# A recurrence of weighted keys and two feed-forward layers: the bonus term moved onto the diagonal of A, and the state product cut into strips of 32

## The chip, the core and the metric

The kernel runs on one core of a Trainium2 chip. The metric is the device time of one execution in microseconds (us); smaller is better. The core has a matrix engine (TensorE, PE in the rows), a vector engine (VectorE, DVE), a scalar engine (ScalarE, ACT), a general one (GpSimd, POOL) and a queue that issues transfers (SyncE, SP). Matrix products land in PSUM, everything else lives in SBUF.

## The reference

Four batches, eight heads, 768 steps, head size 48. For each head a state of 48 x 48 decays, takes up the outer product of the step's key and value, and is read by the step's r. The key and value of the step itself count with a bonus factor u:

```python
for t in range(S):
    cur = np.einsum('bhd,bhe->bhde', u[None] * kt, vt)
    y[:, :, t] = np.einsum('bhd,bhde->bhe', rt, state + cur)
    state = wt[:, :, :, None] * state + np.einsum('bhd,bhe->bhde', kt, vt)
```

The 3072 x 384 result goes through a feed-forward layer, `(h * clip(h + 3, 0, 6) / 6) @ w_out` with `h = x @ w_in` (2048 wide), and then through a second one, `((x @ w1) * (x @ w2)) @ w3 @ w_out` (1024 wide). All is float32.

## The kernel before

**The recurrence by units.** The 768 steps are cut into six chunks of 128. A unit is one chunk of one batch: unit `uu` is chunk `uu // 4` of batch `uu % 4`, 24 units in all. Inside a unit the recurrence is written as products. VectorE scans the decays (`P`, `F`) and scales K and R by them (`K`, `R`). TensorE makes the scores `s` (line 304), K^T R for each of the eight heads, 128 x 128 each, in two PSUM tiles. ScalarE copies them to an SBUF tile A (`a`, `b`, line 311) and GpSimd sets all that isn't strictly above the diagonal to zero (`c`, `d`, line 315). TensorE then adds the outputs of the unit in one PSUM tile (`o`, line 369) from three parts: the state's share R x St, the bonus share, and the share A x V.

**The bonus share.** For the step itself the output gets v times the sum over d of r u k. GpSimd multiplies r by u (`u`, line 402) and by k (`v`, line 404), VectorE sums over d (`l`, line 336: one factor `al` per step and head), GpSimd multiplies V by that (`w`, line 339), and TensorE adds this to the output by a product with the identity (line 377: 12 strips of 32 columns).

**The state.** K is transposed on TensorE (`n`, line 292) and copied (`m`). The state's change is K^T V for each pair of heads (`t`, line 348): one product 112 x 96, of which only the two diagonal blocks of 48 x 48 are used. VectorE adds them to the state (`y`, line 359), which GpSimd decays (`T`).

**Strips.** A product of `o` writes 32 partitions of PSUM, and four in a row write the four quarters. A float32 product stands as two instructions in the trace.

**The first feed-forward layer** runs with the units of the recurrence: block `G` is 9 products of 512 columns (lines 182 to 184) for one of 16 slices of one chunk, `E`, `M`, `H`, `L` are its relu on ScalarE, its product on VectorE, the copy of its high part on ScalarE and the rest on GpSimd (line 451), and `B` is 9 products with w_out. For the first 16 slices the weights are also converted on the way (`a`, `d`, `i`, `p`; lines 166, 170, 796, 802).

**Order.** Nothing is scheduled: the table `ORDER` is a list of such letters, and each engine's queue holds its part of it in that order. PSUM tiles named `wk` rotate through three buffers, so the fourth `wk` tile waits until the first was read. After the table the rest of layer one, a product of w3 and w_out, and layer two follow (phases that the change doesn't touch).

Of the kernel before, what the change touches and what calls it, by code (L numbers as in the profile page):

```python
# [8 lines left out]
F32 = mybir.dt.float32  # L9
# [3 lines left out]
BF16 = mybir.dt.bfloat16  # L13
FP16 = mybir.dt.float16
U16 = mybir.dt.uint16
ALU = mybir.AluOpType
ACTF = mybir.ActivationFunctionType
PSUM = bass.MemoryType.PSUM
# [4 lines left out]
def kernel(  # L23
# [15 lines left out]
    nc = tc.nc  # L39
# [7 lines left out]
    H, D = u.shape  # L47
    DM, NT = out.shape
    G, UPB, BP, C = rT.shape
    S = UPB * C  # L50
    B = NT // S
    NP = H // 2
# [13 lines left out]
    NB2 = NT // N2  # L66
    LAG = 2
    ORDER = (
# [30 lines left out]
    )  # L99
    NST = 3  # L100
    KA = 13
    LO1 = 2
    NZ = 2
    ZC = 2 * DM
    X1F = 13
    LO = 'w0 k0 r0 w1 k2 r1 w3 k1 n0 n3 r2 w2 k3 n1 r3 n2 s0'
    XE = 'ppv'
    XP = (14, 15, 15)
    XL = 13
# [5 lines left out]
    const = ctx.enter_context(tc.tile_pool(name="const", bufs=1))  # L115
# [2 lines left out]
    c_all = const.tile([128, NU, NP], F32, name="c_all")  # L118
    ones = const.tile([128, 1], F32, name="ones")
    flag = const.tile([1, 1], I32, name="flag")  # L120

    main = ExitStack()
    st_p = ctx.enter_context(tc.tile_pool(name="stage", bufs=NST))
# [6 lines left out]
    def pst(tag):  # L130
        return ps.tile([128, 512], F32, tag=tag, name=tag, bufs={"h": 2, "acc": 3, "wk": 3}[tag])
# [8 lines left out]
    wt = wkv.enter_context(tc.tile_pool(name="wk_t", bufs=1, side="right"))  # L140
# [58 lines left out]
    nat3 = ep.tile([128, 2 * DM + VW], F32, name="nat3")  # L199
    qT = [ep.tile([128, FL], F32, name=f"q{q}") for q in range(2)]  # L200
    ubk = ep.tile([128, H], F32, name="ubk")
    St = [wp.tile([128, NP, 2 * D], F32, name=f"St{b}") for b in range(B)]
    xT = {}
    U = [{} for _ in range(NU)]
# [46 lines left out]
    def unit(uu):  # L251
# [3 lines left out]

        d = U[uu]
        c, b = divmod(uu, B)
        first, last = c == 0, c == UPB - 1
        W, kt, rt = (t[own(uu)] for t in (Wb, Kb, Rb))
        kh, rh = (t.rearrange("p (a c) -> p a c", a=NP) for t in (kt, rt))  # L260
        rows = lambda t: t.rearrange("p (m c) -> p m c", c=C)
# [51 lines left out]
        def a_mask(h2):  # L313
            A = d["A"][:, :, h2]
            nc.gpsimd.affine_select(out=A, in_=A, compare_op=ALU.is_ge, fill=0.0, base=-1, pattern=[[0, NP], [1, C]],  # L315
                                    channel_multiplier=-1)

        def q_t():
            nc.gpsimd.tensor_tensor(qT[uu % 2][0:G], kt[0:G], rt[0:G], op=ALU.mult)

# [21 lines left out]
            nc.gpsimd.tensor_tensor(St[b][0:G], St[b][0:G], cs.unsqueeze(2).to_broadcast([G, NP, 2 * D]), op=ALU.mult)  # L342

        def state():
            d["pu"] = pst("acc" if first else "wk")
            for pr in range(NP):
                ds = slice(pr * 2 * D, (pr + 1) * 2 * D)
                nc.tensor.matmul(d["pu"][0:G, ds].rearrange("p (j e) -> p j e", j=2), d["kn"][:, pr, :], d["nv"][:, :, pr, :],  # L348
                                 start=(pr == 0), stop=(pr == NP - 1), skip_group_check=True)
            release("n", uu)  # L350

        def state_add():
            pv = d.pop("pu")[:, 0:DM].rearrange("p (a e) -> p a e", e=2 * D)
            for h2 in range(2):
                rs, es = slice(64 * h2, 64 * h2 + D), slice(h2 * D, (h2 + 1) * D)
                if first:
                    nc.scalar.activation(out=St[b][rs, :, es], in_=pv[rs, :, es], func=ACTF.Copy)
                else:
                    nc.vector.tensor_tensor(St[b][rs, :, es], St[b][rs, :, es], pv[rs, :, es], op=ALU.add)

        def outputs():


            px = d["px"] = pst("wk")
            seen = set()

            def strip(q, lhs, rhs):
                m, j = divmod(q, 4)
                nc.tensor.matmul(px[32 * j:32 * j + 32, m * C:(m + 1) * C], lhs, rhs, start=j not in seen, stop=False, skip_group_check=True)  # L369
                seen.add(j)  # L370

            if not first:
                for q in range(3 * NP):
                    pr, i = divmod(q, 3)
                    strip(q, St[b][0:G, pr, 32 * i:32 * i + 32], rh[0:G, pr, :])
            for q in range(3 * NP):
                strip(q, flat(d["nr"])[:, 32 * q:32 * q + 32], ident)
            for q in range(3 * NP):
                pr, i = divmod(q, 3)
                strip(q, d["v64"][:, i // 2, pr, (0, 32, 32)[i]:(32, 64, 64)[i]],  # L380
                      d["A"][:, pr, i // 2])
            for pr in range(NP):
                strip(3 * pr + 1, d["v64"][:, 1, pr, 0:32], d["A"][:, pr, 1])
            load_r(after(uu))
            release("n", uu)

        def x_split(part):
# [7 lines left out]
                nc.vector.tensor_tensor(xl, pxv, xh.bitcast(F32), op=ALU.subtract)  # L395

        G_, V_ = nc.gpsimd, nc.vector
        return {
            "P": scan_p, "K": lambda: mul_k(V_), "k": lambda: mul_k(G_), "F": scan_f, "R": lambda: mul_r(V_),
            "r": lambda: mul_r(G_), "n": k_t, "m": k_n, "s": scores, "a": lambda: a_copy(0), "b": lambda: a_copy(1),  # L400
            "c": lambda: a_mask(0), "d": lambda: a_mask(1),
# [3 lines left out]
            "V": lambda: V_.tensor_tensor(d["nr"], d["nr"], d["nk"], op=ALU.mult),  # L405
            "q": q_t, "e": q_alpha, "l": alpha, "w": q_bonus if first else bonus, "T": decay, "t": state, "y": state_add, "o": outputs,
            "g": lambda: x_split(0), "h": lambda: x_split(1)}


    wio_t = [[wio_p.tile([128, KA, 2 * DM], F32R, name="wio" + q) for q in "hl"]]  # L410
# [397 lines left out]
    if True:  # L808
# [7 lines left out]
        nc.scalar.activation(out=ones, in_=ones, func=ACTF.Copy)  # L816
        nc.gpsimd.memset(Dp, 0.0)
        nc.gpsimd.memset(Df, 0.0)
        for t in Wb:
            nc.gpsimd.memset(t[0:G, PAD - 1:PAD], 0.0)  # L820
        for t in St:
# [30 lines left out]
        last = NB - 1  # L852
# [135 lines left out]
```

## Time and profile before

| | |
|---|---|
| median of 3 runs | 887.28 us (886.37 to 887.92) |
| profiled execution | 888.7 us, of which the span from first to last instruction is 887.0 us |
| TensorE busy | 865.2 us, 98% of the span |
| GpSimd, VectorE, ScalarE busy | 375.8, 357.5, 330.5 us |
| granted TensorE clock | 0.994 of full speed over the span |
| the units and the table `ORDER` | from the start to about 500 us |

Busy times are shares of one execution. Products overlap on TensorE, so the distance between the starts of two products tells what one costs, not its duration.

### The profile page before, as it was taken

The page shows a single profiled execution, that of the slowest core. Times are in us where ns is not written, and L with a number is a line of the kernel's source. Part 1 is how long each engine was busy: PE and PEld are TensorE (multiplying, and loading weights), DVE is VectorE, ACT ScalarE, POOL GpSimd, SP SyncE. Part 2 cuts the span into 40 slices and gives each one's busy share as a digit, 9 for nine tenths or more (in the row PEclk, how much of TensorE's full clock was granted, in tenths as well). Part 3 has the DMA queues.
Part 4 walks back from the last instruction along what each step waited for, and adds up shares of the span by engine and source line. Part 5 has one row for each costly group of instructions (what it writes and reads, how often), then busy time and mean ns, then how long its engine had stood idle before and what let it go on. Part 6 is the DMA issues. An engine that isn't in the chain of part 4 may idle for free.

```text
span 887.0 us, 13899 instructions
## 1 busy us (share of the span) xinstructions
PE 865.2 (98%) x5752; PEld 707.5 (80%) x5752; DVE 357.5 (40%) x537; ACT 330.5 (37%) x556; POOL 375.8 (42%) x337
## 2 busy tenths in 40 slices
PE   7999999999999999999999999899999999999997
PEld 6777677888888888888888888688888888888785
DVE  7799884444444444444213444155111111212110
ACT  1666633333333333343335555365222222222211
POOL 6677877464555555455232211224232222323221
PEclk9999999999999999999999999999999999999999
DMA  9756541212322122221203452560110404030001
GB/s 257 240 193 229 179 123 46 62 62 62 97 62 75 59 86 66 83 81 53 65 1 108 136 176 85 178 212 2 48 45 1 154 1 155 1 133 1 36 1 39
DMA packets 29239, 81.92 MB, mean 92 GB/s; under 512 B 3312, under 2 KB 3440, under 8 KB 29168
## 3 DMA queue, kind: packets, MB, share of 16 engines
q1 hardware_dynamic: 29168, 80.95, 27.9%
q8 instruction: 47, 0.77, 0.3%
q14 instruction: 24, 0.20, 0.1%
HBM read 71.50 MB, written 9.44 MB: 91 GB/s over the span
## 4 chain that ended last, share of the span: by engine, by line
PE 78%; issue 12%; POOL 5%; DVE 3%; ACT 1%; DMA 0%; SPq 0%; POOLq 0%; ACTq 0%; DVEq 0%
PE h L182 9%; PE acc L183 9%; PE acc L182 9%; PE acc L184 9%; PE h L184 9%; PE h L183 9%; PE wk L369 5%; PE wk L183 4%; PE wk L184 4%; PE wk L182 4%; POOL gl L451 4%; PE wk L304 3%; PE wk L348 1%; PE wk L292 1%; POOL A L315 1%
## 5 line engine op out<-in xcount | busy, mean ns | idle before, releaser
L451 POOL TENSOR_TENSOR gl<-t,gh 128x512 fp32r<-128x512 f32 x144 | 192.0, 1334 | 390.6 <-ACT gh L447 390.5
L447 ACT ACTIVATE gh<-t 128x512 fp32r<-128x512 f32 x144 | 91.0, 632 | 193.1 <-DVE t L606 105.9
L440 DVE SCALAR_TENSOR_TENSOR t<-t,h 128x512 f32<-128x512 f32 x96 | 65.3, 681 | 136.2 <-ACT t L435 135.8
L606 DVE TENSOR_TENSOR t<-t,wk 128x512 f32<-128x512 f32 x48 | 33.0, 687 | 202.9 <-PE wk L184 202.9
L435 ACT ACTIVATE t<-h 128x512 f32<-128x512 f32 x96 | 57.3, 597 | 136.8 <-PE h L184 125.1
L182 PE MATMUL h<-xh,wioh 128*128 128x512 f32 x234 | 94.9, 406 | 0.3 <-DVE t L440 0.3
L182 PE MATMUL acc<-gh,wioh 128*128 128x512 f32 x234 | 93.1, 398 | 0.0
L183 PE MATMUL acc<-gl,wioh 128*128 128x512 f32 x234 | 91.6, 392 | 1.0 <-POOL gl L451 1.0
L184 PE MATMUL h<-xh,wiol 128*128 128x512 f32 x234 | 92.2, 394 | 0.3 <-DVE wiol L802 0.3
L183 PE MATMUL h<-xl,wioh 128*128 128x512 f32 x234 | 91.7, 392 | 0.0
L184 PE MATMUL acc<-gh,wiol 128*128 128x512 f32 x234 | 91.4, 391 | 0.0
L605 ACT ACTIVATE t<-h 128x512 f32<-128x512 f32 x48 | 28.6, 596 | 99.6 <-PE h L184 99.6
L183 PE MATMUL acc<-gl,w34h 128*128 128x512 f32 x144 | 56.3, 391 | 0.0
L184 PE MATMUL acc<-gh,w34l 128*128 128x512 f32 x144 | 56.3, 391 | 0.0
L182 PE MATMUL acc<-gh,w34h 128*128 128x512 f32 x144 | 56.2, 390 | 0.0
L182 PEld LDWEIGHTS h<-xh,wioh 128*128 128x128 f32 x234 | 44.0, 188 | 11.7 <-issue 1.3
L184 PEld LDWEIGHTS h<-xh,wiol 128*128 128x128 f32 x234 | 43.9, 188 | 11.1 <-DVE wiol L802 1.3
L183 PEld LDWEIGHTS acc<-gl,wioh 128*128 128x128 f32 x234 | 44.0, 188 | 10.5 <-POOL gl L451 1.6
L184 PEld LDWEIGHTS acc<-gh,wiol 128*128 128x128 f32 x234 | 43.9, 188 | 9.5
L182 PEld LDWEIGHTS acc<-gh,wioh 128*128 128x128 f32 x234 | 44.0, 188 | 9.4 <-issue 0.2
L166 ACT ACTIVATE z<-st 128x768 f16<-128x768 bf16 (+2 forms) x46 | 41.2, 902 | 27.0 <-DVE st L170 8.5
L183 PEld LDWEIGHTS h<-xl,wioh 128*128 128x128 f32 x234 | 44.0, 188 | 8.5
(141 smaller groups left out, 1727.0 us busy)
## 6 DMA issues: line engine op xcount, KB each, us to landing
nat<-in_rkv_dram SPq DMA_DIRECT2D x20, 640.0 KB, 3.9
st<-in_wio_dram SPq DMA_DIRECT2D x16, 768.0 KB, 4.7
st<-in_w3T_dram SPq DMA_DIRECT2D x16, 512.0 KB, 4.4
W<-in_wT_dram SPq DMA_DIRECT2D x24, 224.0 KB, 2.7
K<-in_kT_dram SPq DMA_DIRECT2D x24, 224.0 KB, 2.6
R<-in_rT_dram SPq DMA_DIRECT2D x24, 224.0 KB, 3.0
st<-in_wT_dram SPq DMA_DIRECT2D x12, 448.0 KB, 6.0
x1d<-ev SPq DMA_DIRECT2D x18, 256.0 KB, 2.9
```

The lines of the kernel that those rows point to most:

```text
L166: nc.scalar.activation(out=z.bitcast(FP16).rearrange("p (n two) -> p n two", two=2)[:, :, 1], in_=half, func=ACTF.Copy)
L182: nc.tensor.matmul(ps_ap, lh, rh, start=first, stop=False)
L183: nc.tensor.matmul(ps_ap, lh, rl, start=False, stop=False)
L184: nc.tensor.matmul(ps_ap, ll, rh, start=False, stop=last)
L304: nc.tensor.matmul(d["sc"][h2][:, pr * C:(pr + 1) * C], kh[sl, pr, :], rh[sl, pr, :], start=(pr == 0), stop=(pr == NP - 1), skip_group_che ...
L369: nc.tensor.matmul(px[32 * j:32 * j + 32, m * C:(m + 1) * C], lhs, rhs, start=j not in seen, stop=False, skip_group_check=True)
L435: nc.scalar.activation(out=t, in_=hp[:, 0:N1], func=ACTF.Relu, bias=3.0)
L440: nc.vector.scalar_tensor_tensor(t, t, 6.0, hp[:, 0:N1], op0=ALU.min, op1=ALU.mult)
L447: nc.scalar.activation(out=gh, in_=t, func=ACTF.Copy)
L451: nc.gpsimd.tensor_tensor(gl, t, gh.bitcast(F32), op=ALU.subtract)
L605: nc.scalar.activation(out=a, in_=pp[0][:, 0:N2], func=ACTF.Copy)
L606: nc.vector.tensor_tensor(a, a, pp[1][:, 0:N2], op=ALU.mult)
```

## The change

The change has three parts.

First, for units 7 to 23 (`DG = 7`) the bonus factors go onto the diagonal of A. GpSimd fills the whole tile A with one select, which puts `al` on the diagonal and zero elsewhere (`c`, `a_diag`). VectorE then copies the scores over it where a constant mask `tri` is one, that is strictly above the diagonal, straight from PSUM (`a` and `b`, `a_over`). In these units the copies `a`, `b` on ScalarE, the two masks on GpSimd, the product `w` on GpSimd and the 12 identity strips of `o` are gone. Units 0 to 6 keep the old way.

Second, in all units the state's change `t` is computed by strips: for each pair of heads four products of 32, 16, 32 and 16 rows by 48 columns in place of one of 112 x 96.

Third, `ORDER` is new. From unit 6 on `t` of one unit, `o` of the next and `s` of the one after stand next to each other on TensorE, and `n` stands alone between two blocks. In the early part some of the work also changes its engine (`r0` moves to GpSimd, `r6` and `r7` move to VectorE), and the order of the first loads is another.

```diff
-        'K21 G R21 L P22 B E u22 M F22 H G v22 L l22 B E M T22 H w22 G L B E M H G L B E M H s20 V L V G V a20',
+        'L o17 y16 s18 g17 h17 G a18 b18 B E u19 M v19 H n17 G L m17 l19 c19 B E M H G K19 L R19 P20 B E M T20',
...
+    DG = 7
...
-    LO = 'w0 k0 r0 w1 k2 r1 w3 k1 n0 n3 r2 w2 k3 n1 r3 n2 s0'
+    LO = 'w0 k0 r0 r1 k1 w1 r2 w2 n0 k2 w3 n1 n2 r3 k3 n3 s0'
...
+        def a_diag():
+
+            d["A"] = wt.tile([128, NP, 2, C], F32, tag="A", name="A", bufs=2)
+            A = d["A"].rearrange("p a j c -> p (a j) c")
+            nc.gpsimd.affine_select(out=A, in_=d["al"].unsqueeze(2).to_broadcast([128, H, C]), compare_op=ALU.is_equal, fill=0.0, base=0,
+                                    pattern=[[0, H], [1, C]], channel_multiplier=-1)
+
+        def a_over(h2):
+
+            nc.vector.copy_predicated(d["A"][:, :, h2], tri.unsqueeze(1).to_broadcast([128, NP, C]),
+                                      d["sc"][h2].rearrange("p (a c) -> p a c", c=C))
...
             for pr in range(NP):
-                ds = slice(pr * 2 * D, (pr + 1) * 2 * D)
-                nc.tensor.matmul(d["pu"][0:G, ds].rearrange("p (j e) -> p j e", j=2), d["kn"][:, pr, :], d["nv"][:, :, pr, :],
-                                 start=(pr == 0), stop=(pr == NP - 1), skip_group_check=True)
+                for j in range(4):
+                    r0, r1 = 32 * j, (32, 48, 96, 112)[j]
+                    nc.tensor.matmul(d["pu"][r0:r1, pr * D:(pr + 1) * D], d["kn"][:, pr, r0:r1], d["nv"][:, j // 2, pr, :],
+                                     start=(pr == 0), stop=(pr == NP - 1), skip_group_check=True)
...
-            for q in range(3 * NP):
+            for q in range(0 if diag else 3 * NP):
                 strip(q, flat(d["nr"])[:, 32 * q:32 * q + 32], ident)
...
+        if diag:
+            ops.update(a=lambda: a_over(0), b=lambda: a_over(1), c=a_diag)
```

What moves is seen in the queues. On TensorE, before, around unit 17: the scores `s` (L304), the outputs `o` (L369) with `n` (L292) behind them, and the state's change `t` (L348) stand in three places, with blocks `G` (h<-) and `B` (acc<-) between them.

```order
L184 MATMUL acc<-gh,wiol 128x512
L304 MATMUL wk<-R_106,K_104 128x128 x8
L182 MATMUL h<-xh,wioh 128x512
...
L184 MATMUL acc<-gh,wiol 128x512
L369 MATMUL wk<-R_106,St_121 32x128 x12
L369 MATMUL wk<-ident,nat 32x128 x12
L369 MATMUL wk<-A,nat 32x128 x16
L292 MATMUL wk<-ident,K_104 128x112 x4
L182 MATMUL h<-xh,wioh 128x512
...
L348 MATMUL wk<-nat,kn 112x96 x4
L182 MATMUL acc<-gh,wioh 128x512
```

After the change (lines are those of the changed program: L364 is `t`, L385 `o`, L306 `s`) the same place of unit 17 reads so; the two rows of L364 stand eight times in turn.

```order
L185 MATMUL acc<-gh,wiol 128x512
L364 MATMUL wk<-nat,kn 32x48
L364 MATMUL wk<-nat,kn 16x48
...
L385 MATMUL wk<-R_107,St_123 32x128 x12
L385 MATMUL wk<-A,nat 32x128 x16
L306 MATMUL wk<-R_106,K_104 128x128 x8
L183 MATMUL h<-xh,wioh 128x512
```

The strips of unit 16's `t`, unit 17's `o` without its identity strips, and unit 18's `s` now follow each other with nothing between.

On VectorE, before, around the same unit: the split `h` (L395) of unit 17's output, then its `y` (L359), a product `M` (L440), and K, R and the scan P of the next unit.

```order
L395 TENSOR_TENSOR xl<-wk,xh 128x3x128
L359 TENSOR_TENSOR St_121<-St_121,wk 48x4x48 x2
L440 SCALAR_TENSOR_TENSOR t<-t,h 128x512
L278 TENSOR_TENSOR K_104<-K_104,P 112x4x127
L284 TENSOR_TENSOR R_106<-R_106,W_102 112x512
```

After the change `y` of unit 16 (L375) stands ahead of `h` of unit 17 (L411), and two masked copies of unit 18's scores (L329) follow.

```order
L274 SCALAR_TENSOR_TENSOR P<-W_103,Dp 112x512
L271 TENSOR_REDUCE c_all<-P 112x4
L276 RECIPROCAL Df<-c_all 112x4
L459 SCALAR_TENSOR_TENSOR t<-t,h 128x512
L283 SCALAR_TENSOR_TENSOR W_103<-W_103,Df 112x512
L459 SCALAR_TENSOR_TENSOR t<-t,h 128x512
L375 TENSOR_TENSOR St_122<-St_122,wk 48x4x48 x2
L411 TENSOR_TENSOR xl<-wk,xh 128x3x128
L329 COPY_PREDICATED A<-tri,wk 128x4x128 x2
```

What moved there: the read of `t`'s PSUM tile now comes while TensorE is at `o`, and the second score tile of `s` takes over that very buffer.

## Rows read from the trace of the kernel before

**Rows 1.** The page: busy times, and the chain that ended last.

```profile
PE 865.2 (98%) x5752; PEld 707.5 (80%) x5752; DVE 357.5 (40%) x537; ACT 330.5 (37%) x556; POOL 375.8 (42%) x337
...
PE 78%; issue 12%; POOL 5%; DVE 3%; ACT 1%; DMA 0%; SPq 0%; POOLq 0%; ACTq 0%; DVEq 0%
```

**Rows 2.** Timeline of TensorE, unit 17: start, duration, line, operation, count.

```profile
329.34 0.39 PE L184 MATMUL acc<-gh,wiol 128*128 128x512 f32 x1
329.66 1.16 PE L304 MATMUL wk<-R,K 48*128 48x128 f32 x16
330.75 0.50 PE L182 MATMUL h<-xh,wioh 128*128 128x512 f32 x1
331.09 0.39 PE L183 MATMUL h<-xl,wioh 128*128 128x512 f32 x1
...
334.52 0.39 PE L183 MATMUL acc<-gl,wioh 128*128 128x512 f32 x1
334.74 0.39 PE L184 MATMUL acc<-gh,wiol 128*128 128x512 f32 x1
335.06 0.86 PE L369 MATMUL wk<-R,St 112*32 112x128 f32 x24
335.74 0.84 PE L369 MATMUL wk<-ident,nat 128*32 128x128 f32 x24
336.40 1.06 PE L369 MATMUL wk<-A,nat 128*32 128x128 f32 x32
337.38 0.60 PE L292 MATMUL wk<-ident,K 112*128 112x112 f32 x4
337.76 0.48 PE L182 MATMUL h<-xh,wioh 128*128 128x512 f32 x1
338.07 0.39 PE L183 MATMUL h<-xl,wioh 128*128 128x512 f32 x1
...
339.68 0.39 PE L184 MATMUL h<-xh,wiol 128*128 128x512 f32 x1
339.91 0.93 PE L348 MATMUL wk<-nat,kn 128*112 128x96 f32 x8
340.63 0.48 PE L182 MATMUL acc<-gh,wioh 128*128 128x512 f32 x1
340.95 0.39 PE L183 MATMUL acc<-gl,wioh 128*128 128x512 f32 x1
```

**Rows 3.** Timeline of TensorE, a transpose that stands alone between products.

```profile
49.40 0.39 PE L184 MATMUL acc<-gh,wiol 128*128 128x512 f32 x1
49.63 0.55 PE L292 MATMUL wk<-ident,K 112*128 112x112 f32 x4
...
50.26 0.39 PE L183 MATMUL acc<-gl,wioh 128*128 128x512 f32 x1
```

**Rows 4.** Busy time by stretch: us, PE, PEld, DVE, ACT, POOL, clock, DMA.

```profile
39.00:60.00 21.00, 20.95 (x183) 16.92 (x181) 18.64 (x23) 15.70 (x25) 14.94 (x12) 1.00 0.58 188
...
80.00:100.00 20.00, 18.37 (x164) 14.12 (x162) 18.97 (x22) 11.82 (x17) 14.51 (x13) 1.00 0.57 188
100.00:120.00 20.00, 18.68 (x160) 14.68 (x161) 16.56 (x21) 11.44 (x17) 15.08 (x12) 1.00 0.39 135
...
158.00:180.00 22.00, 22.00 (x195) 18.15 (x194) 9.57 (x16) 7.57 (x14) 11.93 (x12) 1.00 0.20 62
```

**Rows 5.** Groups by line: operation, count, busy us, mean ns, idle before.

```profile
L606 DVE TENSOR_TENSOR t<-t,wk 128x512 f32<-128x512 f32 x48 | 33.0, 687 | 202.9 <-PE wk L184 202.9
...
L284 DVE TENSOR_TENSOR R<-R,W 112x512 f32<-112x512 f32 x22 | 18.2, 829 | 0.0
...
L315 POOL TENSOR_SCALAR_AFFINE_SELECT A<-A 128x512 f32<-128x512 f32 x48 | 38.1, 816 | 10.0 <-ACT A L311 9.9
```

**Rows 6.** Timeline of VectorE after unit 17's state product.

```profile
340.88 0.72 DVE L359 TENSOR_TENSOR St<-St,wk 48x192 f32<-48x192 f32 x2 [2.27 <-PE wk L348]
```

**Rows 7.** Longest single wait of TensorE, 39 to 140 us: total, times, longest.

```profile
PE wk L369 <- POOL nat L339: 1.3, 1, 1.3
```

More of the change, by code (lines that the diff above doesn't have):

```diff
@@ L15 @@
 U16 = mybir.dt.uint16
+U8 = mybir.dt.uint8
 ALU = mybir.AluOpType
@@ L120 @@
     flag = const.tile([1, 1], I32, name="flag")
+    tri = const.tile([128, C], U8, name="tri")
     main = ExitStack()
@@ L201 @@
     ubk = ep.tile([128, H], F32, name="ubk")
+    pre = ep.tile([128, C], F32, name="pre")
     St = [wp.tile([128, NP, 2 * D], F32, name=f"St{b}") for b in range(B)]
@@ L257, in unit @@
         c, b = divmod(uu, B)
-        first, last = c == 0, c == UPB - 1
+        first, last, diag = c == 0, c == UPB - 1, uu >= DG
         W, kt, rt = (t[own(uu)] for t in (Wb, Kb, Rb))
@@ L346, in state @@
             for pr in range(NP):
-                ds = slice(pr * 2 * D, (pr + 1) * 2 * D)
-                nc.tensor.matmul(d["pu"][0:G, ds].rearrange("p (j e) -> p j e", j=2), d["kn"][:, pr, :], d["nv"][:, :, pr, :],
-                                 start=(pr == 0), stop=(pr == NP - 1), skip_group_check=True)
+                for j in range(4):
+                    r0, r1 = 32 * j, (32, 48, 96, 112)[j]
+                    nc.tensor.matmul(d["pu"][r0:r1, pr * D:(pr + 1) * D], d["kn"][:, pr, r0:r1], d["nv"][:, j // 2, pr, :],
+                                     start=(pr == 0), stop=(pr == NP - 1), skip_group_check=True)
             release("n", uu)
         def state_add():
-            pv = d.pop("pu")[:, 0:DM].rearrange("p (a e) -> p a e", e=2 * D)
+            pv = d.pop("pu")[:, 0:NP * D].rearrange("p (a e) -> p a e", e=D)
             for h2 in range(2):
@@ L356, in state_add @@
                 if first:
-                    nc.scalar.activation(out=St[b][rs, :, es], in_=pv[rs, :, es], func=ACTF.Copy)
+                    nc.scalar.activation(out=St[b][rs, :, es], in_=pv[rs], func=ACTF.Copy)
                 else:
-                    nc.vector.tensor_tensor(St[b][rs, :, es], St[b][rs, :, es], pv[rs, :, es], op=ALU.add)
+                    nc.vector.tensor_tensor(St[b][rs, :, es], St[b][rs, :, es], pv[rs], op=ALU.add)
         def outputs():
@@ L397, in unit @@
         G_, V_ = nc.gpsimd, nc.vector
-        return {
+        ops = {
             "P": scan_p, "K": lambda: mul_k(V_), "k": lambda: mul_k(G_), "F": scan_f, "R": lambda: mul_r(V_),
@@ L407, in unit @@
             "g": lambda: x_split(0), "h": lambda: x_split(1)}
+        if diag:
+            ops.update(a=lambda: a_over(0), b=lambda: a_over(1), c=a_diag)
+        return ops
     wio_t = [[wio_p.tile([128, KA, 2 * DM], F32R, name="wio" + q) for q in "hl"]]
@@ L818 @@
         nc.gpsimd.memset(Df, 0.0)
+        nc.gpsimd.memset(pre, 1.0)
+        nc.gpsimd.affine_select(out=pre, in_=pre, compare_op=ALU.is_ge, fill=0.0, base=-1, pattern=[[1, C]], channel_multiplier=-1)
+        nc.gpsimd.tensor_copy(tri, pre)
         for t in Wb:
```

56 rows, old and new, of the table ORDER are left out of this document.

## The prediction

> **What bounds the kernel now.** I read the page first. TensorE is busy for 865.2 of 887.0 us, no other engine for over 376 us, and TensorE leads the chain that ended last [rows 1]. What TensorE is no longer asked to do therefore comes off the time, unless it then waits for something. So the second view is TensorE's timeline over one unit, where I read distances between starts. In the body of a block two products of 512 columns start 0.22 to 0.23 us apart (334.52 to 334.74); I take 0.227. The small products of a unit stand in three places, and at each I take the distance from the last large product before to the second large one behind, less two large products (0.454), which charges the changeovers too [rows 2]:
>
> - `s`: 329.34 to 331.09 is 1.75, less 0.454 is 1.30 us. Its 16 instructions take 1.09 (329.66 to 330.75); entering costs 0.09 (0.32 instead of 0.227), leaving 0.11 (0.34 instead of 0.227).
> - `o` and `n`: 334.74 to 338.07 is 3.33, less 0.454 is 2.88 us: entry 0.09, state share 0.68 (24 instructions), identity strips 0.66 (24), A share 0.98 (32, with the changeover behind it), `n` 0.38, leaving about 0.08.
> - `t`: 339.68 to 340.95 is 1.27, less 0.454 is 0.82 us: 0.72 for eight instructions (339.91 to 340.63), no extra at entry, 0.09 to 0.10 behind.
>
> The third view is the busy time by stretch. In three stretches of the early part VectorE is busy for 18.64 us of 21, 18.97 of 20 and 16.56 of 20, 83 to 95%, beside a TensorE that works 58.0 of these 61 us; from 158 us on VectorE works 9.57 of 22 us and TensorE all 22 [rows 4]. So there are two regimes: early, TensorE and VectorE bind together, later TensorE alone.
>
> **The change part by part.**
>
> *Identity strips.* 17 units lose 24 instructions each, 0.66 us as measured between the starts at 335.74 and 336.40 [rows 2]: 17 x 0.66 = 11.2 us off TensorE.
>
> *The state's strips.* Each `t` had 8 instructions and now has 32, since each of its 16 products stands as two. No row of before shows a strip with 48 moving columns. The upper row is `s`, which keeps two products in the array side by side: 1.09/16 = 0.068 us each, so 32 take 2.18 us. The lower bound lets the time go with the columns moved and all four quarters at once: 8 x 96 columns take 0.72 us, 32 x 48 spread over four quarters are half of that, 0.36 us. Nearest are the strips of `o`: the same 32-wide target, four in turn, two instructions each. 24 take 0.66 to 0.68 us, 0.028 each, though they move 128 columns [rows 2]. I take that price and don't reckon with a gain from 48 columns: 32 x 0.0275 = 0.88 us. Against 0.82 before (0.72 and its exit of 0.10; the exit goes, since `t` is followed by `o`) that is +0.06 for each of the 17 `t` that stand on TensorE's path (units 3 to 19): +1.0 us. The bounds are 17 x (0.36 - 0.82) = -7.8 and 17 x (2.18 - 0.82) = +23 us.
>
> One rule speaks against the strips. The rows of `o` show 0.028 us from one small instruction to the next. The Trainium skill ("TensorE: Matmul & The Clock Gate", section "Wait — 56ns, not 53.3ns?") says that starts never come closer than about 25 ns however few columns move, and that without hardware decode each matmul costs about 62 ns. By the first, 32 strips can't go under 0.80 us, close to what I take; by the second they would cost 1.98 us and the change would lose some 20 us on `t`. The trace rules the second out here, for 62 ns can't hold beside 28.
>
> *Adjacency.* Before, `s` and `o` each paid an entry of 0.09. Now one group `t`, `o`, `s` pays one. About 14 groups: -1.3 us. `n` cost 0.38 + 0.11 behind `o`; alone between large products it costs 49.40 to 50.26 less 0.454, 0.41 us [rows 3]: some 14 x 0.08 = -1.1 us.
>
> *Work on the other engines.* Per unit VectorE gains two masked copies from PSUM. The trace has none; the nearest row is a 512-column operation with one operand in PSUM, 687 ns, so 1.4 us; 0.83 us each would be the price of that width with both operands in SBUF, and nothing is the bound from below. GpSimd loses `w` and two masks of 816 ns and gains one select of twice their width, some 1.6 us [rows 5]; ScalarE loses two copies. Beyond 158 us VectorE has 12 us free in 22 [rows 4], so there this costs nothing. If the cover were gone, it would be 1.4 us per unit. `c` is issued nearly a unit ahead of the scores that are copied over it, and a wait for it would be VectorE's.
>
> *New waits.* With three `wk` buffers the second score tile of `s` takes the buffer of `t`. `s` thus can't pass its first product until `y` has read `t`. Before, `y` began 0.25 us after the end of `t` (340.63 to 340.88) and took 0.72 us, done 0.97 us after `t` [rows 6]. Between `t` and `s` stands `o` without its identity strips, 0.68 + 0.98 = 1.66 us. Some 0.7 us are left, and ahead of `y` on VectorE stand a scan and an `M` whose inputs come from blocks that ended 2 us or more before. I count zero.
>
> *The early part.* TensorE's idle time in those three stretches is 3.0 us [rows 4]; its longest wait, 1.3 us, is for `w` of unit 7 [rows 7], which the change removes. GpSimd gets lighter. VectorE gets R of units 6 and 7 (2 x 0.83 [rows 5]) and the masked copies of units 7 and 8 (4 x 0.69): +4.4 us on an engine that is 83 to 95% busy there. The units also come earlier against the blocks, with less TensorE work between them, so VectorE may end last. I set the loss equal to the gain, zero, with bounds of -3 (these waits gone) and +5 us (VectorE's extra work all on the path). In the first 39 us the new order lets the third scan of VectorE run ahead but puts one more multiplication on GpSimd: zero, give or take 1 us.
>
> **Sum.** -11.2 + 1.0 - 1.3 - 1.1 = -12.6 us. From the profiled execution, 888.7 us with a span of 887.0, this gives 876.1. That execution lies 1.4 us above the median of 887.28, so against the median it is 874.7 us.
>
> **Rivals.**
> 1. *The early part turns into a VectorE bound* and keeps 5 of the 12.6 us: about 880. For it speaks VectorE's 83 to 95%, against it that VectorE's work for the later blocks comes no later than before and GpSimd's load falls.
> 2. *Short strips are cheap*, 0.36 us, or the early waits vanish: 3 to 9 us more, 866 to 872. Against it stands the even 0.028 us of three kinds of strips.
> 3. *`s` waits for `y`* (the other side): VectorE's queue delays `y` in every group. It takes 0.7 us of lateness before a wait begins, and with 14 groups each further 0.9 us costs 12.6; if `y` is 1.8 us late each time, the time is 874.7 + 14 x 1.1 = 890. For it: the scan of P has two operands in SBUF and takes longer than the `y` itself. Against it: VectorE was idle for over half of the time there [rows 4].
> 4. *The strips of `t` run no closer than the products of `s`*: 17 x 1.3 = 22 us more, about 897. Against it: `o`'s strips have the same form. The skill's 62 ns would give about 893.
>
> **How the numbers follow.** Forecast 0.70, rival 1 0.13, rival 2 0.09, rival 3 0.04, rival 4 0.04. The range of 866.5 to 882.5 takes in the forecast, nearly all of rivals 1 and 2, and leaves rivals 3 and 4 and a tail of rival 1 outside. What a measurement of this kernel tells from no change is about 0.2%, 1.8 us. Faster by more than that (below 885.5) is the forecast with rivals 1 and 2, less a tail: 0.91. Within it 0.03, slower 0.06 (rivals 3 and 4 with most of their weight).
>
> **What would show it.** In the changed kernel's timeline around 330 us the 32 strips of `t` should take 0.8 to 0.9 us, `o` 1.66 and `s` 1.09, with no wait row of `s` for VectorE's `y`. 17 x 24 identity instructions should be gone. VectorE's busy share up to 140 us should stay above 90%, and TensorE's waits there should sum to about what they did. The masked copy should take near 0.7 us. The prediction is wrong if the group `t`, `o`, `s` takes clearly more than 3.7 us, or if the waits before 140 us grow by more than 5 us.

## The result, and the profile after

The changed kernel takes 852.69 us (median of 4 runs, 852.08 to 854.18), the kernel before in the same session 887.39 us: a ratio of 0.9606 (0.9587 to 0.9625), 34.7 us faster. The forecast was 874.7 with a range of 866.5 to 882.5, so the time fell below the range; the sign was right and the gain was nearly three times the forecast's 12.6 us.

The page after, its busy times and the chain that ended last (beside [rows 1]):

```profile
PE 833.3 (98%) x5819; PEld 689.5 (81%) x5819; DVE 389.1 (46%) x572; ACT 311.6 (37%) x522; POOL 347.8 (41%) x305
...
PE 74%; issue 15%; POOL 6%; DVE 3%; DMA 1%; SPq 0%; ACT 0%; POOLq 0%
```

TensorE still bounds the kernel. It lost 31.9 us of busy time, although it runs more instructions than before.

TensorE's timeline after, the group of unit 16's `t` (L364), unit 17's `o` (L385) and unit 18's `s` (L306), and below it an `n` (L294) that stands alone (start, duration, line, operation, count, as in [rows 2]):

```profile
311.01 0.39 PE L185 MATMUL acc<-gh,wiol 128*128 128x512 f32 x1
311.33 0.54 PE L364 MATMUL wk<-nat,kn 128*32 128x48 f32 x32
311.69 0.84 PE L385 MATMUL wk<-R,St 112*32 112x128 f32 x24
312.34 1.06 PE L385 MATMUL wk<-A,nat 128*32 128x128 f32 x32
313.33 1.16 PE L306 MATMUL wk<-R,K 48*128 48x128 f32 x16
314.42 0.50 PE L183 MATMUL h<-xh,wioh 128*128 128x512 f32 x1
314.76 0.39 PE L184 MATMUL h<-xl,wioh 128*128 128x512 f32 x1
...
318.42 0.40 PE L185 MATMUL acc<-gh,wiol 128*128 128x512 f32 x1
318.65 0.55 PE L294 MATMUL wk<-ident,K 112*128 112x112 f32 x4
318.97 0.48 PE L183 MATMUL h<-xh,wioh 128*128 128x512 f32 x1
319.29 0.40 PE L184 MATMUL h<-xl,wioh 128*128 128x512 f32 x1
```

The 32 strips of `t` take 0.36 us (311.33 to 311.69), not the 0.88 of the forecast. `o` takes 1.64 and `s` 1.09 us, as said, and the group 3.09 us (311.33 to 314.42). From 311.01 to 314.76, less two products, it costs 3.30 us. `n` alone costs 318.42 to 319.29 less 0.454, 0.42 us; [rows 3] gave 0.41.

VectorE's timeline beside that group (in brackets the idle time ahead and what ended it), `y` and the masked copies:

```profile
311.94 0.72 DVE L375 TENSOR_TENSOR St<-St,wk 48x192 f32<-48x192 f32 x2 [1.17 <-PE wk L364]
...
314.53 1.36 DVE L329 COPY_PREDICATED A<-tri,wk 128x512 f32<-128x512 uint8 x2
```

`y` begins 0.25 us after the end of `t`, the same distance as in [rows 6], and is done at 312.66, 0.67 us ahead of `s` (313.33). The wait of rival 3 does not arise. The masked copy and the select among the groups by line:

```profile
L324 POOL TENSOR_SCALAR_AFFINE_SELECT A<-al 128x1024 f32<-128x1024 f32 x17 | 21.3, 1255 | 2.3 <-DVE Dp L271 1.1 <-DVE al L350 0.7 <-PE wk L385 0.4
L329 DVE COPY_PREDICATED A<-tri,wk 128x512 f32<-128x512 uint8 x34 | 23.1, 729 | 0.0
```

A masked copy takes 729 ns (forecast near 0.7 us), the select 1255 ns (1.6 us). The stretches of [rows 4] after, in the same columns, and the list of TensorE's waits from 39 to 150 us, which has one row:

```profile
39.00:60.00 21.00, 20.03 (x230) 16.27 (x230) 19.86 (x25) 15.62 (x25) 17.76 (x14) 1.00 0.80 270
80.00:100.00 20.00, 19.41 (x204) 15.71 (x200) 19.35 (x30) 12.26 (x18) 17.26 (x13) 1.00 0.81 271
100.00:120.00 20.00, 20.00 (x181) 16.50 (x180) 19.04 (x25) 11.84 (x18) 12.18 (x10) 1.00 0.35 111
158.00:180.00 22.00, 22.00 (x190) 18.07 (x189) 10.89 (x17) 5.97 (x11) 7.73 (x8) 1.00 0.20 61
```

```profile
PE acc L184 <- POOL gl L470: 2.6, 3, 1.0
```

VectorE is now busy 95 to 97% of the three early stretches, and TensorE waits 2.6 us from 39 to 150 us. Before, it waited 3.6 us there: 1.3 us for `w` [rows 7], 0.8 us in three short waits, and 1.5 us for GpSimd's `gl`:

```profile
PE acc L183 <- POOL gl L451: 1.5, 2, 1.0
```

The forecast spoke only of the units. A region that the change doesn't touch also got faster. In layer two, 640 to 840 us, TensorE is busy throughout, and the number of products of 512 columns that start there is not the same (columns: length, TensorE busy and count, clock, DMA share, GB/s); first the kernel before, then after:

```profile
640.00:840.00 200.00, 200.00 (x868) 1.00 0.17 60
```

```profile
640.00:840.00 200.00, 200.00 (x884) 1.00 0.15 53
```

That is 200/868 = 230.4 ns per product before and 226.2 ns after, at the same clock. The first experiments went to this.

### The profile page after: what moved, and what is told of

Same layout as the page of the kernel before. It is cut to its first block, busy times and chain, and to the rows that moved or that the text cites. A ratio compares the mean times of both kernels' runs of the same rounds, so it can differ in the third digit from the quotient of the medians.

```text
span 852.1 us, 14037 instructions
## 1 busy us (share of the span) xinstructions
PE 833.3 (98%) x5819; PEld 689.5 (81%) x5819; DVE 389.1 (46%) x572; ACT 311.6 (37%) x522; POOL 347.8 (41%) x305
## 4 chain that ended last, share of the span: by engine, by line
PE 74%; issue 15%; POOL 6%; DVE 3%; DMA 1%; SPq 0%; ACT 0%; POOLq 0%
PE acc L184 9%; PE acc L185 9%; PE h L183 9%; PE acc L183 9%; PE h L185 9%; PE h L184 9%; POOL gl L470 4%; PE wk L184 4%; PE wk L185 4%; PE wk L183 4%; PE wk L385 4%; PE wk L306 2%; PE wk L364 1%; DVE wiol L821 1%; DMA nat<-in_rkv_dram 1%
## 5 line engine op out<-in xcount | busy, mean ns | idle before, releaser
L470 POOL TENSOR_TENSOR gl<-t,gh 128x512 fp32r<-128x512 f32 x144 | 196.5, 1366 | 402.9 <-ACT gh L466 402.7
```

What stands on the lines that cost most here:

```text
L470: nc.gpsimd.tensor_tensor(gl, t, gh.bitcast(F32), op=ALU.subtract)
```

## Experiments

All ratios are to the kernel before, run on the same chip; their 95% intervals reach 1.2 to 2.6 us to either side. What is called slower or the same as the changed kernel is set against its median of 852.69 us, which was measured ahead of these runs, so a difference of one or two microseconds between two runs says little. Times of TensorE "in the units" are sums of distances between starts, over all rows of its timeline from the first block `G` to unit 23's `o`.

### The placement of the tiles

The mask `tri` takes 128 bytes per partition in the constant pool, and every tile that is allocated after it on the left side of SBUF moves up by 128; tiles on the right side stay. The first two kernels move the tiles and change nothing else.

```diff
+    spare = const.tile([128, 128], mybir.dt.uint8, name="spare")
```

The kernel before with the unused tile:

> The kernel before with one unused tile of 128 bytes a partition among the constants; nothing else is changed, so every tile of the left side lies 128 bytes further, as the mask tri pushes it in the changed kernel. Placement theory: the products of 512 columns run at 0.233 us in layer two and in the even chunks only because the weights (left side) and the moving operand (right side) lie 128 bytes apart modulo 256; the pad undoes that. Layer two shrinks from 300.3 to about 294.4 us, the even chunks by 3 to 4 us, the product of w3 and w_out by under 1 us: about 877 us, ratio 0.988. Rival, timing theory: the pace came from the other engines' work and the order; the pad does nothing: 887.4 us, ratio 1.000.

878.80 us, 0.9908 (0.9892 to 0.9925): 8.1 us faster without a single changed instruction. The changed kernel with the same tile once more, so that the shift is 256:

> The changed kernel with the same unused 128 bytes: its left side now lies 256 bytes from that of the kernel before. Placement theory: layer two goes back from 294.4 to about 300 us and the even chunks lose 3 to 4 us: 862 to 863 us, ratio 0.972 to the kernel before. Timing theory: 852.7 us, ratio 0.961.

860.82 us, 0.9715 (0.9697 to 0.9732): 8.1 us slower than the changed kernel. Layer two from 640 to 840 us shows 868 products again. So 8.1 of the 34.7 us came from the place of the tiles. Half the shift:

```diff
+    spare = const.tile([128, 64], mybir.dt.uint8, name="spare")
```

> The kernel before with 64 unused bytes: weights and right-side operand lie 64 bytes apart modulo 256 in place of 128. If the pace needs them equal, nothing changes: 887 us, and products at 0.231 to 0.233 us in layer two, perhaps in the odd chunks too. If it goes by distance, half the gain of 8.1 us: 883 us.

884.94 us, 0.9973 (0.9959 to 0.9987): 2.9 us faster, in between. Its timeline in layer two shows nine products of `x1` with `w12` (64 bytes apart), nine of `g` with `w34`, and the next:

```profile
663.53 0.39 PE L183 MATMUL wk<-x1h,w12h 128*128 128x512 f32 x1
...
665.59 0.40 PE L183 MATMUL acc<-gh,w34h 128*128 128x512 f32 x1
...
667.68 0.40 PE L183 MATMUL h<-x1h,w12h 128*128 128x512 f32 x1
```

The first nine take 2.06 us. The nine behind them take 2.09 us, although `g` and `w34` both lie on the left side and at the same address modulo 256 (160 in the compiled program). So at a shift of 64 the slow products aren't only those whose own two operands lie apart. Whether the place of the left side counts by itself, or its distance to the right side, was told apart by shifting the right side instead:

```diff
+    spare_p = ctx.enter_context(tc.tile_pool(name="spare", bufs=1, side="right"))
+    spare = spare_p.tile([128, 128], mybir.dt.uint8, name="spare")
```

> The kernel before with an unused 128-byte tile at the outer end of the right side of SBUF: the right-side tiles (x of the even chunks, x of layer two) move down by 128 bytes, every weight and every other tile stays where it is. Theory A, what counts is the distance between the addresses of the weights and of the moving operand, modulo 256: it is 0 again for all products of 512 columns, so the time is that of the kernel with the left-side pad, 878 to 880 us, and products of layer two start 226.7 ns apart. Theory B, what counts is where the left-side tiles lie by themselves: no change, 886 to 888 us. A half gain, 882 to 884, would say that both matter.

880.75 us, 0.9931 (0.9903 to 0.996); the runs spread more than the others (877.93 to 882.73). Layer two from 640 to 840 us, the kernel with the left tile and the kernel with the right one:

```profile
640.00:840.00 200.00, 200.00 (x883) 1.00 0.16 55
```

```profile
640.00:840.00 200.00, 200.00 (x884) 1.00 0.16 56
```

Either shift gives the fast products, so what counts is how the two sides lie to each other, not where the left side lies by itself. The addresses of the compiled programs, in bytes per partition modulo 256:

```
                            before   left +128   right -128   after
w12h, w12l (left)             96        224          96        224
x1h, x1l (right)             224        224          96        224
w12ah, w12al (right)         224        224          96        224
wioh, wiol (left)             96        224          96        224
xh, xl, even chunks (right)  224        224          96        224
xh, xl, odd chunks (left)     96        224          96        224
```

The kernel before shows both cases within 8 us. Its timeline in layer two, `x1` first with the weights `w12a` (right side, like `x1`), then with `w12` (left side); nine products each, of which the first and the one that follows the ninth stand here:

```profile
678.22 0.39 PE L182 MATMUL wk<-x1h,w12ah 128*128 128x512 f32 x1
...
680.26 0.39 PE L182 MATMUL acc<-gh,w34h 128*128 128x512 f32 x1
...
684.40 0.39 PE L182 MATMUL wk<-x1h,w12h 128*128 128x512 f32 x1
...
686.50 0.39 PE L182 MATMUL acc<-gh,w34h 128*128 128x512 f32 x1
```

Where both operands lie at the same address modulo 256, nine products take 2.04 us, 227 ns each. Where they lie 128 apart they take 2.10 us, 233 ns each. This holds for distances of 0 and 128; the run with 64 bytes doesn't fit a rule that looks at one product's two operands alone, and why the addresses matter stays open.

### The state's strips

The strips alone in the kernel before (with the read in `y` fitted to them, and without `tri`, so that nothing moves):

```diff
-                nc.tensor.matmul(d["pu"][0:G, ds].rearrange("p (j e) -> p j e", j=2), d["kn"][:, pr, :], d["nv"][:, :, pr, :],
...
+                for j in range(4):
+                    r0, r1 = 32 * j, (32, 48, 96, 112)[j]
+                    nc.tensor.matmul(d["pu"][r0:r1, pr * D:(pr + 1) * D], d["kn"][:, pr, r0:r1], d["nv"][:, j // 2, pr, :],
```

> The kernel before with the state's product in strips (and its read), old order, old bonus. If a strip's time goes with its columns over four quarters at once, the 32 instructions take 0.36 us; standing between two blocks, t also pays an entry of 0.09 and an exit of 0.12 us: 0.58 us instead of 0.82, 17 times: about -4 us, 883 us. If, as I predicted, they go at the pace of the output's strips (0.028 us each), t costs 0.88 + 0.2: +4 us, 892 us.

883.87 us, 0.9968 (0.9955 to 0.9982): 3.1 us faster. TensorE's timeline there, a `t` that stands alone:

```profile
315.67 0.39 PE L184 MATMUL h<-xh,wiol 128*128 128x512 f32 x1
315.99 0.54 PE L350 MATMUL wk<-nat,kn 128*32 128x48 f32 x32
316.46 0.50 PE L182 MATMUL acc<-gh,wioh 128*128 128x512 f32 x1
316.80 0.40 PE L183 MATMUL acc<-gl,wioh 128*128 128x512 f32 x1
```

Alone it costs 315.67 to 316.80 less 0.454, 0.68 us, against 0.82 before: it pays an entry of 0.09, 0.47 and an exit of 0.11. The strips themselves are cheap; between two blocks the changeovers eat much of it. The reverse, the changed kernel with the whole `t` (the diff above with its signs swapped):

> The changed kernel with the state's product whole again (4 products of 112 x 96 a unit), new order, new bonus. If strips cost 0.36 us against 0.72 us and the exit of the whole product is paid as a changeover into the output's strips: 17 x 0.36 to 0.46 = 6 to 8 us more, 859 to 861 us. If the strips gained nothing (the prediction's price), 852 us.

859.42 us, 0.9695 (0.9674 to 0.9716): 6.7 us slower than the changed kernel. Beside `o` the strips are worth twice what they are worth alone. TensorE's timeline there, the whole `t` (L362) ahead of `o`:

```profile
316.04 0.39 PE L185 MATMUL acc<-gh,wiol 128*128 128x512 f32 x1
316.26 0.93 PE L362 MATMUL wk<-nat,kn 128*112 128x96 f32 x8
317.12 0.86 PE L383 MATMUL wk<-R,St 112*32 112x128 f32 x24
```

The whole `t` costs 0.86 us here and nothing extra at its entry (0.22 us). The strips cost 0.36 and an entry of 0.09, so they save 0.41 us in the group against 0.82 - 0.68 = 0.14 us alone. For 17 units that is an estimate of 7.0 and 2.4 us, where 6.7 and 3.1 were measured.

### The bonus on the diagonal

The diagonal alone in the kernel before, with `tri` and a second 128 bytes, so that the operands lie as before:

```diff
+    DG = 7
+    spare = const.tile([128, 128], mybir.dt.uint8, name="spare")
+    tri = const.tile([128, C], U8, name="tri")
...
-            for q in range(3 * NP):
+            for q in range(0 if diag else 3 * NP):
...
+        if diag:
+            ops.update(a=lambda: a_over(0), b=lambda: a_over(1), c=a_diag)
```

> The kernel before, old order, with the bonus on the diagonal for units 7 to 23 (select right behind the output two units ahead or behind al, whichever is later; w, c, d dropped) and with 128 unused bytes beside the mask, so that the left side lies 256 bytes further and the two sides stand to each other as before. Identity strips alone: 17 x 0.66 = 11.2 us off TensorE, and unit 7's wait of 1.3 us for w: 874 to 876 us, ratio 0.986. If the masked copies on VectorE cost TensorE time early, up to 5 us less of a gain: 880 us.

878.96 us, 0.9908 (0.9885 to 0.993): 8.9 us faster, less than expected. The identity strips fell from 13.39 to 2.22 us in the units, 11.2 us, as the forecast had it, but TensorE now waits longer. Its list of waits from 39 to 160 us:

```profile
PE acc L186 <- POOL gl L470: 3.3, 3, 1.9
PE h L185 <- DVE t L459: 1.9, 2, 1.6
...
```

With two short ones left out here these are 5.7 us, in place of 3.6 in the kernel before. The wait of 1.3 us for `w` is gone, so 2.3 was to be expected; the 3.4 us more are nearly all that is missing from the 12.5 us (11.2 and 1.3). The reverse, the changed kernel with the old bonus in all units (`DG = 99`, and `c`, `d`, `w` back in the order; `tri` stays):

> The changed kernel with the old bonus in all units (w where the select stood, copies on ScalarE, masks on GpSimd behind them, identity strips), new order, strips and placement kept. Identity strips: 17 x 0.66 = 11.2 us, so 864 us, ratio 0.974. More than that, up to 870 us, if TensorE then waits for the masks on GpSimd in the new order.

865.25 us, 0.9748 (0.9727 to 0.9768): 12.6 us slower than the changed kernel.

### The order

All edits but the order, in the old order:

> Old order with everything else of the change: diagonal, strips, and the placement that the mask brings. If the parts add up (placement -8.1, strips in the old order -3.1, diagonal -11 to -12.5 us): 863 to 865 us, ratio 0.974; then the new order is worth about 11 us by itself (adjacent changeovers some 0.2 to 0.3 us in each of 17 groups, and waits before 140 us). If the order is worth only what I predicted for adjacency (2.4 us): 855 us.

868.01 us, 0.9787 (0.9763 to 0.981), above both values. The new order is worth 15.3 us on top. TensorE's waits there from 39 to 150 us (three short ones left out), and its 20 us from 120 to 140:

```profile
PE acc L185 <- POOL gl L471: 3.3, 3, 1.9
PE h L184 <- DVE t L460: 2.7, 2, 2.2
PE h L186 <- DVE wiol L822: 0.7, 2, 0.5
PE wk L295 <- DVE A L330: 0.6, 1, 0.6
...
```

```profile
120.00:140.00 20.00, 16.73 (x182) 13.07 (x181) 18.98 (x30) 4.79 (x9) 14.79 (x14) 1.00 0.39 120
```

In the old order VectorE is busy for 18.98 us of these 20, in the new order for 14.38, and TensorE waits 8.1 us in all, against 2.6 in the new order. Half of the 8.1 are waits for VectorE (the three rows with DVE), the longest row is one for GpSimd. The order by itself, with old bonus and whole `t` (`DG = 99`, the whole `t` as above):

> The changed kernel with the old bonus (identity strips) and the whole t in all units: the new order alone, with the 128 bytes of tri kept in place so that the SBUF addresses are those of the changed kernel. Beside it stands the kernel before with the same 128 bytes, 878.8 us. Theory A, the parts add up: 852.7 + 12.6 (bonus undone) + 6.7 (strips undone) = 872.0, so the order by itself is worth about 7 us. Theory B, the order is worth the same 15.3 us with the old parts as with the new: 878.8 - 15.3 = 863.5. Theory C, all that the order does is to take away waits which the other two edits create: 877 to 879. I expect A: of the 15.3 us about 6 are waits that only arise with the other edits. TensorE's idle time inside the units should be about 2 us, as before.

872.07 us, 0.983 (0.9804 to 0.9856). Beside the kernel with the left tile (878.8) the order alone is worth 6.7 us. Theory A gave 872.0; that it is met to 0.1 us is luck, since the runs don't tell so little apart. Its only row of TensorE's waits from 39 to 150 us:

```profile
PE acc L186 <- POOL gl L470: 1.9, 3, 0.7
```

In the new order the parts add up: bonus and strips undone one at a time cost 12.6 + 6.7 = 19.3 us, undone together 19.4. In the old order the same two are worth only 878.80 - 868.01 = 10.8 us. The waits account for 3.8 us of the 8.6 between: the two edits raise them by 4.5 us in the old order (3.6 to 8.1) and by 0.7 in the new one (1.9 to 2.6). The changeovers of the strips make up most of the rest, 17 x (0.41 - 0.14) = 4.6 us as an estimate.

The adjacency alone undone, in units 8 to 18 (three groups shown, cut):

```diff
-  ... K10 L R10 B E P11 M t8 T11 o9 y8 H F11 L s10 g9 h9 B a10 b10 ...
+  ... K10 L R10 t8 B E P11 M T11 o9 y8 H F11 L g9 h9 B s10 a10 b10 ...
-  ... P12 L B E F12 T12 M t9 H o10 y9 L s11 g10 h10 G a11 b11 ...
+  ... P12 L t9 B E F12 T12 M H o10 y9 L g10 h10 G s11 a11 b11 ...
-  ... P13 G E t10 E M T13 o11 y10 M s12 F13 g11 G h11 a12 ...
+  ... P13 t10 G E E M T13 o11 y10 M F13 g11 G s12 h11 a12 ...
```

> The changed kernel with only the adjacency undone: in eleven groups (units 8 to 18) t stands one block earlier and s one block later in the order, so that t, o and s stand alone between products of 512 columns again. Bonus on the diagonal, strips and placement stay. Theory A, by entries and exits: each group pays two more entries of 0.09 and two more exits of 0.10 to 0.14 us, about 0.4 us, eleven times 4.4 us: 856 to 858. Theory B, t's and s's places matter mainly through early waits, which lie ahead of unit 8: within 1 us of 852.7. If it goes above 860, new waits of s or y arise, which the list of waits would name.

859.39 us, 0.9689 (0.9664 to 0.9714): 6.7 us slower than the changed kernel, 0.6 us per group; theory A by its sign, with a price half as high again. TensorE's timeline there, a `t` and an `o` alone:

```profile
313.88 0.39 PE L186 MATMUL h<-xh,wiol 128*128 128x512 f32 x1
314.20 0.54 PE L365 MATMUL wk<-nat,kn 128*32 128x48 f32 x32
314.67 0.50 PE L184 MATMUL acc<-gh,wioh 128*128 128x512 f32 x1
315.01 0.40 PE L185 MATMUL acc<-gl,wioh 128*128 128x512 f32 x1
...
316.62 0.39 PE L186 MATMUL acc<-gh,wiol 128*128 128x512 f32 x1
316.94 0.86 PE L386 MATMUL wk<-R,St 112*32 112x128 f32 x24
317.62 1.06 PE L386 MATMUL wk<-A,nat 128*32 128x128 f32 x32
318.60 0.50 PE L184 MATMUL h<-xh,wioh 128*128 128x512 f32 x1
318.94 0.40 PE L185 MATMUL h<-xl,wioh 128*128 128x512 f32 x1
```

Alone, `t` costs 0.68 us (313.88 to 315.01), `o` 1.87 (316.62 to 318.94) and `s` 1.30 [rows 2], each less two products: 3.85 us where the group costs 3.30. That is 0.55 us per group, eleven times 6.0 of the 6.7 us. TensorE's waits from 39 to 150 us are 3.0 us there, 0.4 more than in the changed kernel.

### Further in the same direction

The bonus on the diagonal from unit 5, as a version that might beat both (`c5`, `c6` moved ahead of `a5`, `a6`; `d` and `w` of these units gone):

```diff
-    DG = 7
+    DG = 5
```

> The changed kernel with the bonus on the diagonal already from unit 5 (two units more). Theory A: the identity strips of two more units go, 2 x 0.66 = 1.3 us: 851.4. Theory B: VectorE binds there and gets four masked copies of about 0.7 us each more, up to 2.8 us: 854 to 855.5. If both hold in part the time stays within 1 us of 852.7.

853.01 us (851.06 to 853.94), 0.9615 (0.9593 to 0.9637): no difference to the changed kernel that these runs could tell; theory A's 851.4 lies at the edge of the interval. The identity strips of two units are gone from TensorE (1.97 to 0.66 us in the units), but it works 18.48 us of 60 to 80 us with VectorE at 19.83:

```profile
60.00:80.00 20.00, 18.48 (x151) 14.13 (x150) 19.83 (x26) 10.59 (x15) 12.11 (x11) 1.00 0.43 137
```

In the changed kernel the same stretch has 18.96 and also 19.83. From the first block `G` to unit 23's `o` TensorE's timeline is as long as in the changed kernel, 388.9 and 388.8 us, though 1.3 us of products are gone. This speaks for theory B: what TensorE is spared where VectorE is busy all the time doesn't come off. The times alone don't show it. No version beat the changed kernel.

## Why the prediction was wrong

Undone one at a time in the changed kernel, the bonus is worth 12.6, the strips 6.7 and the placement 8.1 us. That leaves 34.7 - 27.4 = 7.3 us to the order, which alone measured 6.7. Three steps of the forecast failed: the price of the strips, the placement that it left at nothing, and the size of the changeovers. Its terms beside what was measured:

- **Identity strips, -11.2 us: right.** TensorE's time for them fell by 11.4 us in the units; undoing it cost 12.6.
- **The state's strips, +1.0 us: the wrong end was taken.** The step that failed here is "I take that price and don't reckon with a gain from 48 columns". They cost 0.36 us, the lower bound of the same paragraph: the columns count. Four instructions of `o`'s state share take 0.65/6 = 0.108 us with 128 columns, four of `t` 0.36/8 = 0.045 us with 48; the ratio is 2.4 where the columns have 2.7. The argument against rival 2, "the even 0.028 us of three kinds of strips", couldn't tell a price by instruction from a price by column, for all three kinds move 128 columns. By the rows of before, 24 x 128 columns over four quarters at the pace of the whole `t` (0.72 us for 8 x 96) make 0.72 us, where `o`'s strips took 0.66 to 0.68: the 0.028 was already the price of the columns. The term is -6.7 us, and the error 7.7. Rival 2 had this case with 0.09, together with the vanishing waits; its 866 to 872 was right on the mechanism and didn't reach the time for the other two reasons. The Trainium skill ("TensorE: Matmul & The Clock Gate", section "Wait — 56ns, not 53.3ns?") was called as a witness with its 25 ns between starts; here 32 starts in 0.36 us lie 11 ns apart on average, and the measurement decides.
- **The placement, not in the sum at all.** This is the largest single error, 8.1 us. The change adds a constant of 128 bytes a partition, the mask `tri`, and the time of layer two, which "the change doesn't touch", was taken as given. The trace of before held the hint: `x1` with `w12a` and with `w12` run at 227 and 233 ns a product.
- **Adjacency and `n`, -1.3 and -1.1 us: right in kind, too small.** The entry of `t` was counted as free, and its exit of 0.10 was booked under the strips, where it was then lost in the higher price. With short strips the changeovers are a large part of `t`: 0.55 us per group by the rows, 0.6 measured, where 0.09 was booked. The order alone is worth 6.7 us instead of 2.4; 1.7 of it are shorter early waits (3.6 to 1.9 us), which the forecast had at zero.
- **The early part, 0 (-3 to +5): right, by luck.** TensorE's waits went from 3.6 to 2.6 us, but not because a loss and a gain are equal, as the forecast had it. In the old order the same edits bring 8.1 us of waits, 4.5 more than before and near the 5 us of rival 1; the new order takes them away.
- **`s` waits for `y`, 0: right**, with the margin of 0.7 us that was worked out. **Masked copies, hidden: right** from unit 7 on, with 729 ns each; for units 5 and 6 the run with `DG = 5` speaks against it.

The errors are 7.7 (strips), 8.1 (placement), 4.9 (order, 7.3 for 2.4) and 1.4 (bonus), 22.1 us in all, which is 34.7 - 12.6. That they close is no check, for the order's 7.3 is what the others leave; with the 6.7 that it measured alone, 0.6 us stay open. The largest single failure is not a price but the scope: the range was made from the edits' own costs, and a change that also moves every later tile of a side can cost or gain in all of the kernel's products.

## What to carry to other kernels

When a change adds or removes a tile, compare the addresses of weights and moving operands before and after, and look for places in the old trace where the same product runs at two speeds; here 128 unused bytes were worth 0.9%. Here the price of small instructions that fill the four quarters in turn went about with the columns that they move (48 against 128), so a product that computes unused blocks could be cut without paying for more instructions, and it paid most beside other small products, where no changeover to a block follows. An order that was right for one balance of engines has to be made anew when work moves from one engine to another: bonus and strips gave 10.8 us in the old order and 19.4 in the new.

## What the runs showed of the hardware

- Products of 512 columns with weights and moving operand 128 bytes apart modulo 256 start 233 ns apart, with both at the same place 227 ns; the 64-byte tile gave a gain of 2.9 in place of 8.1 us, and with it products whose operands lie at the same place were slow too (2.09 us for nine, 232 ns each). Why isn't shown by any row: the granted clock is 1.00 in all of them, and TensorE has no wait there. Distances other than 0, 64 and 128 weren't tried.
- 32 instructions (16 float32 products of 32 or 16 rows by 48 columns), in turn over four quarters, take 0.36 us ahead of `o` and 0.47 us ahead of a block.
- A changeover between the small products and a block costs 0.09 us ahead and 0.11 us behind; at `t` in strips, whose own time ahead of a block is 0.11 us longer as well, this makes 0.32 us (0.68 alone, 0.36 in the group).
